# A streaming kernel's loads issued earlier, and another gate for its first store

## The chip, the cores and the metric

The kernel runs on one core of one Trainium2 chip. The core's VectorE (DVE in the profile) does the arithmetic, SyncE (SP) issues the transfers between HBM and the on-chip memory, and 16 DMA engines carry them out. TensorE (PE) does one tiny matmul; ScalarE does nothing. The metric is the device time of one execution in microseconds (us), the median of several runs.

## The reference

The reference scales one array by a scalar and adds it to another, in bf16:

```python
B, S, D = 512, 32, 640
x, fx: (B, S, D) bf16;  alpha: (1,) bf16
def reference(x, fx, alpha):
    return x + alpha * fx
```

Each array has 10,485,760 elements, 20.97 MB. Two are read and one is written, 62.9 MB in all, with one multiplication and one addition per element.

## The kernel before

All three arrays are seen as 128 partitions by 160 *units* of K = 512 columns (1 KB per partition and unit, so 128 KB per unit). On the chip there is one tile, `room`, with 207 such units per partition (`ROOM`, line 13); x and fx together are 320 units, so places are used more than once. x and the result share a place: the add is done in place.

What is done, and in which order, is written by hand in the string `PLAN` (lines 25 to 50). A loop (line 100) takes its steps in order, and each goes to the end of its engine's own queue: loads and stores to SP's, multiplies and adds to VectorE's. Engines run their queues in order and independently; a step waits on its engine until what it needs is done, and the steps behind it on that engine wait too. The steps are:

- `x a b @ p` or `f a b @ p`: load units a to b of x or fx to place p (line 94);
- `a`: load alpha and spread it to 128 partitions with a matmul (`spread_alpha`, lines 82 to 89);
- `m p n`: multiply the n units at place p by alpha, in place (line 108);
- `+ p q n`: add the n units of fx at place q to the n units of x at place p (line 113);
- `s a b @ p`: store units a to b from place p (line 94). With `after x 128` it also waits until the load of x that starts at unit 128 has landed (lines 95 and 96).

A load into a place that held something else waits for the add that read it last. Before, the loads run in this order: fx 0-64 (in two parts, alpha behind them), x 0-32, x 32-64, fx 64-128, x 64-88, x 88-128, fx 128-160, x 128-152, x 152-160. The first five wait for nothing. x 64-88 goes where the first 24 units of fx lay and so waits for the add of x 0-32; x 88-128 waits for the add of x 32-64; fx 128-160 goes to places 64 to 96 and waits for `+ 143 79 24`; x 128-152 and x 152-160 go to places 96 to 128 and wait for `+ 167 103 25`. The stores, of units 0-64, 64-128 and 128-160, come last; the first has the gate `after x 128`. At the end SP waits for all transfers.

A transfer of 128 partitions is done by all 16 DMA engines, each with eight of the rows; the trace has one packet for each row.

Of the kernel before, what the change touches and what calls it, by code (L numbers as in the profile page):

```python
# [1 line left out]

# [4 lines left out]

ALU = mybir.AluOpType
F32 = mybir.dt.float32

K = 512
P = 128
ROOM = 207

PLAN = """
f 0 8 @ 143
f 8 64 @ 151
a
x 0 32 @ 0
m 143 64  # L30
x 32 64 @ 32
+ 0 143 32
+ 32 175 32
f 64 128 @ 79
m 79 64
x 64 88 @ 143
+ 143 79 24
x 88 128 @ 167
f 128 160 @ 64
+ 167 103 25  # L40
+ 192 128 15
x 128 152 @ 96
x 152 160 @ 120
m 64 32
s 0 64 @ 0 after x 128
+ 96 64 24
s 64 128 @ 143
+ 120 88 8
s 128 160 @ 96
"""  # L50


@with_exitstack
def kernel(
    ctx: ExitStack,
    tc: tile.TileContext,
    x: bass.AP,
    fx: bass.AP,
    alpha: bass.AP,
    out: bass.AP,  # L60
):
    nc = tc.nc
    whole = {
        name: t.flatten_outer_dims().rearrange("(p n) d -> p (n d)", p=P)
        for name, t in (("x", x), ("f", fx), ("s", out))
    }
    assert whole["x"].shape[1] == 160 * K

    consts = ctx.enter_context(tc.tile_pool(name="consts", bufs=1))
    psum = ctx.enter_context(tc.tile_pool(name="psum", bufs=1, space=bass.MemoryType.PSUM))  # L70
    rooms = ctx.enter_context(tc.tile_pool(name="rooms", bufs=1))
    ctx.enter_context(tc.manual_schedule())

    room = rooms.tile([P, ROOM * K], x.dtype, name="room")
    a_f = consts.tile([P, 1], F32, name="a_f")
    info = mybir.DependencyInfo(mybir.DependencyClass.Sync, mybir.DependencyReason.DATA)
    done, moved = [], {}

    def units(t, a, b):
        return t[:, a * K : b * K]  # L80

    def spread_alpha():
        a_1 = consts.tile([1, 1], alpha.dtype, name="a_1")
        done.append(nc.sync.dma_start(out=a_1[:], in_=alpha[None, :]))  # L84
        ones = consts.tile([1, P], alpha.dtype, name="ones")
        nc.vector.memset(ones[:], 1.0)  # L86
        a_ps = psum.tile([P, 1], F32, name="a_ps")
        done.append(nc.tensor.matmul(a_ps[:], ones[:], a_1[:], start=True, stop=True))  # L88
        nc.vector.tensor_copy(out=a_f[:], in_=a_ps[:])  # L89

    def transfer(what, a, b, at, after):
        away, here = units(whole[what], a, b), units(room, at, at + b - a)
        out, in_ = (away, here) if what == "s" else (here, away)
        r = nc.sync.dma_start(out=out, in_=in_)  # L94
        if after:
            tc.add_manual_dep(r.ins, moved[after].ins.name, info, reason="issued late")
        moved[what, a] = r
        done.append(r)

    for step in PLAN.strip().split("\n"):  # L100
        what, *rest = step.split()
        if what == "a":
            spread_alpha()
        elif what == "m":
            t, n = map(int, rest)
            f = units(room, t, t + n)
            done.append(
                nc.vector.tensor_scalar(out=f, in0=f, scalar1=a_f[:], scalar2=None, op0=ALU.mult)  # L108
            )
        elif what == "+":  # L110
            t, u, n = map(int, rest)
            xt, f = units(room, t, t + n), units(room, u, u + n)
            done.append(nc.vector.tensor_tensor(out=xt, in0=xt, in1=f, op=ALU.add))  # L113
        else:
            a, b, _, at = rest[:4]
            after = (rest[5], int(rest[6])) if len(rest) > 4 else None
            transfer(what, int(a), int(b), int(at), after)

    last = nc.sync.nop(nofuse=True)
    for i in done[:-1]:  # L120
        tc.add_manual_dep(last.ins, i.ins.name, info, reason="all but the last store")


# [1 line left out]
_INS = ['x', 'fx', 'alpha']  # L125
_OUTS = [((512, 32, 640), 'bfloat16')]


# [23 lines left out]
```

## Time and profile before

| | us |
|---|---|
| median of 3 runs (lowest, highest) | 152.31 (152.21, 152.66) |
| the profiled execution | 152.51 |
| its span in the profile | 150.7 |
| busy in the span: VectorE | 65.8 (44%) |
| adds: 128x16384 / 128x12288 / 128x4096 | 8.693 / 6.559 / 2.284 each |
| multiplies: 128x32768 / 128x16384 | 8.752 / 4.480 each |
| moved: read / written | 41.94 MB / 20.97 MB, 417 GB/s over the span |

The span is the stretch that the profiler records; the device time has some 1.8 us more around it. Times in the profile are counted from the span's start. In the profile's rows SPq is SP's queue, "room<-in_x_dram" a load of x, "out_dram<-room" a store, and a bracket at the end of a row tells how long the engine stood idle before it and what ended that. Rows of the timeline merge neighbours of a kind: "x2" with a length can span two instructions that lie apart.

### The profile page before, as it was taken

The numbers are of one execution on the slowest core, as the hardware profiler recorded it, in microseconds if no ns is written. First come the engines' busy times: TensorE is split into PE (matmuls) and PEld (weight loads), VectorE is DVE, ScalarE is ACT, GpSimd is POOL, SyncE is SP. The second block draws the span as 40 slices with busy tenths as digits, with TensorE's granted clock in tenths as the row PEclk, the third lists the DMA queues.
The fourth block names the chain that finished last, engine by engine and source line by source line (L and its number), as shares of the span: only waits on it lengthen the run. The fifth ranks groups of instructions, "written<-read, shape, count | busy, mean of one in ns | idle before, by whom it ended". The sixth has DMA issues, their size and how long they took to land.

```text
span 150.7 us, 83 instructions
## 1 busy us (share of the span) xinstructions
PE 0.2 (0%) x1; PEld 0.1 (0%) x1; DVE 65.8 (44%) x12; POOL 0.2 (0%) x4
## 2 busy tenths in 40 slices
PE   0000000000000000000000000000000000000000
PEld 0000000000000000000000000000000000000000
DVE  0000009979889400799935999479500000000000
POOL 0000000000000000000000000000000000000000
DMA  5997989999969696999999999999799697979992
GB/s 170 596 411 320 487 383 426 435 461 461 565 296 557 278 557 285 437 489 424 435 435 417 417 389 430 400 450 504 330 504 557 296 539 330 504 330 391 417 478 104
DMA packets 1874, 62.92 MB, mean 417 GB/s; under 512 B 210, under 2 KB 210, under 8 KB 210
## 3 DMA queue, kind: packets, MB, share of 16 engines
q1 hardware_dynamic: 1874, 62.92, 97.3%
HBM read 41.94 MB, written 20.97 MB: 417 GB/s over the span
## 4 chain that ended last, share of the span: by engine, by line
DMA 54%; DVE 15%; DVEq 1%; SPq 1%; issue 0%
DMA room<-in_x_dram 54%; DVE room L113 15%; DVEq L147 1%; SPq L94 1%; SPq L84 0%; DVEq L113 0%
## 5 line engine op out<-in xcount | busy, mean ns | idle before, releaser
L113 DVE TENSOR_TENSOR room<-room 128x16384 bf16<-128x16384 bf16 (+4 forms) x7 | 43.6, 6252 | 8.8 <-DMA room<-in_x_dram 8.8
L108 DVE TENSOR_SCALAR room<-room,a_f 128x32768 bf16<-128x32768 bf16 (+1 forms) x3 | 22.0, 7328 | 10.7 <-DMA room<-in_fx_dram 10.7
L89 DVE COPY a_f<-a_ps 128x1 f32<-128x1 f32 x1 | 0.2, 159 | 21.5 <-PE a_ps L88 21.5
L86 DVE MEMSET ones<- 1x128 bf16 x1 | 0.2, 165 | 0.8 <-PEq L136 0.8
L88 PE MATMUL a_ps<-a,ones 1*128 1x1 bf16 x1 | 0.2, 158 | 22.3 <-DMA a<-in_alpha_dram 22.3
L136 POOL MEMSET const-bfloat16-1.0<- 128x1 bf16 x1 | 0.1, 102 | 0.0
L136 POOL MEMSET const-uint8-127<- 128x1 uint8 x1 | 0.1, 102 | 0.0
L88 PEld LDWEIGHTS <-ones 1*128 1x128 bf16 x1 | 0.1, 101 | 1.0 <-DVE ones L86 1.0
L136 POOL MEMSET const-float32-0.0<- 128x1 f32 x1 | 0.1, 99 | 0.2 <-issue 0.2
L136 POOL MEMSET const-float32-1.0<- 128x1 f32 x1 | 0.1, 99 | 0.0
## 6 DMA issues: line engine op xcount, KB each, us to landing
room<-in_x_dram SPq DMA_DIRECT2D x2, 4096.0 KB, 34.8
room<-in_fx_dram SPq DMA_DIRECT2D x1, 7168.0 KB, 21.3
room<-in_x_dram SPq DMA_DIRECT2D x2, 3072.0 KB, 19.4
room<-in_x_dram SPq DMA_DIRECT2D x1, 5120.0 KB, 30.0
room<-in_fx_dram SPq DMA_DIRECT2D x1, 4096.0 KB, 13.8
out_dram<-room SPq DMA_DIRECT2D x1, 4096.0 KB, 42.3
room<-in_fx_dram SPq DMA_DIRECT2D x1, 1024.0 KB, 4.8
room<-in_x_dram SPq DMA_DIRECT2D x1, 1024.0 KB
```

The lines of the kernel that those rows point to most:

```text
L86: nc.vector.memset(ones[:], 1.0)
L88: done.append(nc.tensor.matmul(a_ps[:], ones[:], a_1[:], start=True, stop=True))
L89: nc.vector.tensor_copy(out=a_f[:], in_=a_ps[:])
L94: r = nc.sync.dma_start(out=out, in_=in_)
L108: nc.vector.tensor_scalar(out=f, in0=f, scalar1=a_f[:], scalar2=None, op0=ALU.mult)
L113: done.append(nc.vector.tensor_tensor(out=xt, in0=xt, in1=f, op=ALU.add))
L136: nc = _bacc.Bacc("TRN2", target_bir_lowering=False, num_devices=1)
L147: with _tile.TileContext(nc) as tc:
```

## The change

Only the order and the division of the steps change; the places, the bytes and the arithmetic are the same.

- x 0-64 is loaded in one transfer instead of two.
- The adds of x 0-64 become 24, 16 and 24 units, and behind each the load into the place that it frees is issued: x 64-88, x 88-104, x 104-128 (before: 24 and 40 units, behind adds of 32 and 32).
- The adds of x 64-128 become 17, 7, 16, 9, 9 and 6 units (before 24, 25 and 15). fx 128-160 waits for the one of 17 units. x 128-160 is one load (before two) and waits for those of 7, 16 and 9; the last 9 + 6 units come behind the multiply of fx 128-160.
- The first store waits for the add `+ 192 128 9` instead of the landing of x 128-152; to allow this, adds are recorded in `moved` as transfers are.
- The last adds, of 24 and 8 units, become one of 32.

```diff
 a
-x 0 32 @ 0
+x 0 64 @ 0
 m 143 64
-x 32 64 @ 32
-+ 0 143 32
-+ 32 175 32
 f 64 128 @ 79
++ 0 143 24
+x 64 88 @ 143
++ 24 167 16
+x 88 104 @ 167
++ 40 183 24
+x 104 128 @ 183
 m 79 64
-x 64 88 @ 143
-+ 143 79 24
-x 88 128 @ 167
++ 143 79 17
 f 128 160 @ 64
-+ 167 103 25
-+ 192 128 15
-x 128 152 @ 96
-x 152 160 @ 120
++ 160 96 7
++ 167 103 16
++ 183 119 9
+x 128 160 @ 96
 m 64 32
-s 0 64 @ 0 after x 128
-+ 96 64 24
++ 192 128 9
+s 0 64 @ 0 after + 192
++ 201 137 6
 s 64 128 @ 143
-+ 120 88 8
++ 96 64 32
 s 128 160 @ 96
...
-            done.append(nc.vector.tensor_tensor(out=xt, in0=xt, in1=f, op=ALU.add))
+            moved[what, t] = nc.vector.tensor_tensor(out=xt, in0=xt, in1=f, op=ALU.add)
+            done.append(moved[what, t])
```

## The prediction

> **What bounds the kernel now.** I read the page first: busy shares, the DMA slices, the queue, the chain of waits.
>
> ```profile
> span 150.7 us, 83 instructions
> PE 0.2 (0%) x1; PEld 0.1 (0%) x1; DVE 65.8 (44%) x12; POOL 0.2 (0%) x4
> DMA  5997989999969696999999999999799697979992
> q1 hardware_dynamic: 1874, 62.92, 97.3%
> DMA 54%; DVE 15%; DVEq 1%; SPq 1%; issue 0%
> ```
>
> VectorE works 44% of the span; the 16 DMA engines are occupied 97.3% of it. So only time in which a DMA engine stands idle or is slow can be won, and the chain's 15% of VectorE matters only where an engine ran dry behind it. The question is where the missing 2.7% lies. Then the timeline, for the moments at which SP issues transfers and what releases them:
>
> ```profile
> 41.01 9.98 SPq L94 DMA_DIRECT2D room<-in_x_dram  x2
> 61.28 8.75 DVE L108 TENSOR_SCALAR room<-room,a_f 128x32768 bf16<-128x32768 bf16 x1 [10.65 <-DMA room<-in_fx_dram]
> 76.65 0.33 SPq L94 DMA_DIRECT2D room<-in_fx_dram  x1
> 80.71 10.89 DVE L113 TENSOR_TENSOR room<-room 128x12800 bf16<-128x12800 bf16 x2 [4.08 <-DMA room<-in_x_dram]
> 87.56 0.80 SPq L94 DMA_DIRECT2D room<-in_x_dram  x2
> 98.80 9.20 SPq L94 DMA_DIRECT2D out_dram<-room  x3
> 98.88 8.76 DVE L113 TENSOR_TENSOR room<-room 128x12288 bf16<-128x12288 bf16 x2 [2.88 <-DMA room<-in_x_dram]
> ```
>
> x 64-88 (41.01) and x 88-128 (50.66, merged into the first row) are issued long before fx 64-128 has landed at 61.3. But fx 128-160 goes out at 76.65, while its turn comes at 79.6-80.2, and x 128-152 at 87.56 for a turn at 89.4-90.0. Last, DMA shares by window (a packet counts where it starts; last columns are clock, DMA share, GB/s):
>
> ```profile
> 41.00:60.00 19.00, 0.00 (x0) 0.00 (x0) 8.69 (x1) 0.00 (x0) 1.00 1.00 435
> 89.30:91.30 2.00, 0.00 (x0) 0.00 (x0) 2.00 (x1) 0.00 (x0) 1.00 0.95 381
> 98.80:99.30 0.50, 0.00 (x0) 0.00 (x0) 0.42 (x1) 0.00 (x0) 1.00 0.91 360
> 148.50:149.70 1.20, 0.00 (x0) 0.00 (x0) 0.00 (x0) 0.00 (x0) 1.00 0.00 0
> ```
>
> With a deep queue the engines give 435 GB/s; around 90 and 99 they fall short; after 148.5 no packet starts any more though the last ends at 149.64. The trace's single packets (one row of a transfer each; I chained each packet to the one that ended just before it) say who falls short:
>
> ```
>                       13 engines        3 engines
> fx 128-160 ends       89.38-89.96       89.58, 89.62, 89.67
> x 128-152 starts      2 ns later        90.22, 90.47, 90.51; first packet 1.47-1.63, others 0.91
> x 152-160 ends        99.15-99.8        about 101.0, 101.28, 101.32
> first store starts    99.64-99.80       100.99, 101.29, 101.32
> last store has landed 148.49-148.68     149.63, 149.95, 149.98
> ```
>
> Three engines found no descriptors of x 128-152 when they were done with fx 128-160: 0.6-0.9 us of idleness and a first packet 0.56-0.72 us too long, 1.3 to 1.5 us in all. They never make it up, since no engine has spare time afterwards, and the kernel ends with them, 1.30 us (149.98 - 148.68) after the other 13. These 13 lost less: they ran out of loads up to 0.64 us before the first store, which waited for x 128-152 to land (98.78) and went out at 98.80.
>
> **The change, part by part.** The profiled execution took 152.51 us, span 150.7 and 1.8 around it; the median of the runs is 152.31, 0.20 lower, so differences are taken in the span and put on 152.31.
>
> Prices of an add: 128x16384 took 8.693 and 128x4096 took 2.284, so 0.148 us plus 0.5216 ns per column: 6.56 for 24 units of 512, 4.69 for 17, 4.42 for 16, 2.55 for 9, 2.02 for 7, 1.75 for 6. Multiplies: 8.75 for 64 units, 4.48 for 32. Seven adds become ten: 3 x 0.148 = 0.44 us more on VectorE, which is idle over half the span.
>
> *x 0-64 in one load.* One issue less at 2.4 (0.56 us of SP), behind fx 8-64, which keeps the engines busy to 22: no effect there. But the first add can no longer start at 32.29 with half of x; it starts when all has landed, at 41.9. From there: 24 units to 48.5, 16 to 52.9, 24 to 59.5. So x 64-88, 88-104 and 104-128 are issued at 48.5, 52.9, 59.5; their turns come at 60.2, 67.5 and 72.3. The cover is fx 64-128, in flight to 61.3: leads of 11.7 us and more, where 3.5 (below) are the most that was needed, so the later first add may slip 8 us more before it costs.
>
> *fx 128-160 and x 128-160.* The multiply of fx 64-128 starts at 61.28 as now (VectorE free at 59.5), ends 70.0; 17 units to 74.7: fx 128-160 is issued at 74.7 instead of 76.65, lead 4.9 us instead of 3.0. Then 7 units to 76.8, 16 to 81.2, 9 to 83.8 (x 104-128 lands at 80.7, in time): x 128-160 is issued at 83.8 instead of 87.56, lead 5.6 us instead of 1.8. The small delays at the start of fx 128-160 now (one gap of 0.10, two first packets 0.17 too long) fall on engines that end with the 13 or are swallowed in the later stall, so that lead is worth 0 to 0.1. Both leads, 4.9 (the thinnest margin) and 5.6 us, exceed the longest delay seen from issue to an undisturbed rate: x 128-152 in the three engines, (90.51 + 0.56) - 87.56 = 3.5 us. So this stall goes: 1.30 us for the end of the three.
>
> *The gate of the first store.* fx 128-160 lands at 90.4 as now; its multiply ends at 94.9, the gating add of 9 units at 97.5, and SP issues the store then, 1.3 us earlier than now and 1.6 to 2.1 us before the engines run out of loads (99.1-99.65: 9.7 us after 89.4-89.96). Queued behind the gate on SP are only the other two stores: the second wants the 6 units that end at 99.3, the third the last add, from about 100.1 to 108.8; the queue then holds 64 units of stores each time (the second store's own last landing is 140 now), so neither is missed. What the 13 engines lose now (0 to 0.64 idle, first store packets 2.48 instead of 2.42) goes or stays at 0.06. The price of a late descriptor for a store issued into full reading is in no row: bounds below.
>
> *Packets.* x 0-64 and x 128-160 need 8 packets per engine less each, x 64-128 8 more; one packet of 65536 B took 2.418 against 2 x 1.215: 0.012 us each, 8 fewer are 0.1 us at most; I take 0.05.
>
> Sum: -1.30 (three engines) - 0.1 (part of what the 13 lose; the last of them found its store with no gap, so between 0 and 0.2) - 0.05 = -1.45 us. 152.31 - 1.45 = 150.86.
>
> **Bounds of the unknown price.** Store descriptors now: the 13 engines that stood waiting began 0.84 to 1.0 us after the issue, and the other three found theirs ready when they wanted them, 2.2 to 2.5 us after it. With 1.6-2.1 us of lead this is a stall of 0 to 0.5. The upper end is the load of 87.56, whose three late engines began 2.66-2.95 us after the issue and were at full rate after 3.4-3.5: 97.5 + 2.7..3.5 against the 99.35 in the middle is 0.8 to 1.65. I take 0, since a store's own rows are nearer than a load's; both ends go into the range.
>
> **The rivals.**
> *The store's wait takes the load's place.* The lead of the first store (1.6-2.1) is that of x 128-152 now (1.8-2.4), at the same full reading. If three engines are as late for it, 0.8 to 1.65 of the 1.45 come back: 151.66 to 152.5. Against it: the store rows above.
> *The lag has nothing to do with the lead* (it hangs on the addresses of x 128, or on three of the engines): then x 128-160 stalls all the same and only the 0.05 and the earlier store remain: about 152.2. For it: 13 engines had their descriptors within 1.8 us. Against it: the 3.0 us lead of fx 128-160 left only 0.1-0.17, leads of 19 us and more left nothing, and the three engines' later packets are as short as the others'.
> The Trainium skill speaks for this rival (DMA: Bandwidth & Descriptors, "Latency and other measured facts"): about 0.6 us to the first byte of a transfer issued by SP, by which 1.8 us of lead would be enough and the early issue would buy nothing. The trace disagrees for the three engines (2.66 us and more); the same section's 2 us of HBM latency under high load, added to 0.6 as an estimate, comes to 2.6.
> *Slower: the gated store comes too late.* The gate hangs on the landing of fx 128-160 plus 7.1 us of VectorE, with everything else already issued. If descriptors of a store issued among full reads need more than 97.5 to 101.3 = 3.8 us on some engine, the end is as late as now or later; at 4.5 us, 150.86 + (102.0 - 99.35) = 153.5. For it: nothing that long is seen; against it: 3.5 is the longest.
>
> **How the numbers follow.** A measurement here can tell about 0.3% (0.46 us): faster is below 151.85, slower above 152.77. Forecast 0.53 (own range 150.6-151.4); store's wait 0.25, half of it below 151.85; lag without the lead 0.11; slower 0.11. Faster 0.53 + 0.12 = 0.65, same 0.13 + 0.11 = 0.24, slower 0.11. The range 150.6 to 152.4 leaves out the last case and the far end of the second.
>
> **What would show it.** In the profile after: x loads issued at 48.5, 52.9, 59.5, fx at 74.7, x 128-160 at 83.8, first store near 97.5; all 16 engines starting x 128-160 without a gap near 89.4-90; the last landings of all within 0.6 us of each other near 148.5, the span near 149.3. Wrong would be: gaps in some engines after 99.1 (the store), or a first packet of x 128-160 of over 1.3 us (the lag without the lead), or VectorE still adding when a load's turn comes.

## The result, and the profile after

The changed kernel takes 150.82 us (median of 4 runs, 150.75 to 150.87); the kernel before, with one more run beside it, 152.49 (152.21 to 152.90). The ratio is 0.9888, with a 95% interval of 0.9862 to 0.9914: faster by about 1.1%. The forecast was 150.86. The profiled execution took 150.81 us, its span 149.0, against 152.51 and 150.7.

The page of the changed kernel, the same parts as were shown of before (busy time, DMA share of 40 slices, the queue, the chain that ended last):

```profile
span 149.0 us, 85 instructions
PE 0.2 (0%) x1; PEld 0.1 (0%) x1; DVE 65.9 (44%) x15; POOL 0.2 (0%) x4
DMA  5997996969899796999998999999696969697994
q1 hardware_dynamic: 1730, 62.92, 98.1%
DMA 38%; DVE 32%; another core or an unknown queue 1%; SPq 1%; issue 0%; DVEq 0%
```

The bytes are the same and the DMA engines' share of the span rises from 97.3 to 98.1%. VectorE's part of the chain doubles, 15% to 32%, while the kernel gets faster. The chain follows who released whom, and the first store is now released by an add; that doesn't mean that any DMA engine waited for this add. Whether an engine ran dry is seen only in the DMA records.

The timeline of the changed kernel, the moments of issue (start, length, queue, transfer):

```profile
41.70 17.36 DVE L115 TENSOR_TENSOR room<-room 128x12288 bf16<-128x12288 bf16 x3 [10.34 <-DMA room<-in_x_dram]
48.29 11.13 SPq L96 DMA_DIRECT2D room<-in_x_dram  x3
61.00 8.75 DVE L110 TENSOR_SCALAR room<-room,a_f 128x32768 bf16<-128x32768 bf16 x1 [1.94 <-DMA room<-in_fx_dram]
74.51 0.33 SPq L96 DMA_DIRECT2D room<-in_fx_dram  x1
83.25 0.33 SPq L96 DMA_DIRECT2D room<-in_x_dram  x1
97.25 11.86 SPq L96 DMA_DIRECT2D out_dram<-room  x3
```

VectorE starts adding 9.4 us later than before, and it costs nothing: its three adds are done 1.94 us before fx 64-128 has landed. fx 128-160 goes out at 74.5 and x 128-160 at 83.25, 5 and 6 us ahead of their turns.

Windows, first of before and then of the changed kernel, over the stretch in which x 128-160 is read (last columns: clock, DMA share, GB/s):

```profile
89.30:99.10 9.80, 0.00 (x0) 0.00 (x0) 6.92 (x3) 0.00 (x0) 1.00 0.97 407
```

```profile
89.30:99.10 9.80, 0.00 (x0) 0.00 (x0) 8.62 (x3) 0.00 (x0) 1.00 1.00 428
148.50:149.70 1.20, 0.00 (x0) 0.00 (x0) 0.00 (x0) 0.00 (x0) 1.00 0.00 0
```

407 GB/s became 428 there: the short windows of the prediction (2 us and less) are no good for a comparison, because a packet counts where it starts and a whole row of 16 may fall on either side of an edge. After 148.5 no packet starts in either kernel; only the records of single packets tell how long the last ones run. Those of the changed kernel, in the form of the prediction's table:

```
                      all 16 engines
fx 128-160 ends       89.39-89.73
x 128-160 starts      at most 4 ns later; first packet 1.21-1.25, in one engine 1.44
x 128-160 ends        99.13-99.61
first store starts    at most 4 ns later; first packet 2.42 (once 2.44)
last store has landed 147.84-148.27
```

Between 5 us and its end no engine is idle for more than 0.08 us at a time, and no group of three lags: the last landings lie within 0.43 us where they lay within 1.49.

### The profile page after: what moved, and what is told of

It reads as the page before. It is cut to its first block, busy times and chain, and to the rows that moved or that the text cites. A ratio compares the mean times of both kernels' runs of the same rounds, so it can differ in the third digit from the quotient of the medians.

```text
span 149.0 us, 85 instructions
## 1 busy us (share of the span) xinstructions
PE 0.2 (0%) x1; PEld 0.1 (0%) x1; DVE 65.9 (44%) x15; POOL 0.2 (0%) x4
## 3 DMA queue, kind: packets, MB, share of 16 engines
q1 hardware_dynamic: 1730, 62.92, 98.1%
## 4 chain that ended last, share of the span: by engine, by line
DMA 38%; DVE 32%; another core or an unknown queue 1%; SPq 1%; issue 0%; DVEq 0%
DMA room<-in_x_dram 38%; DVE room L115 27%; DVE room L110 6%; SPq L96 1%; SPq L86 0%; DVEq L115 0%
## 5 line engine op out<-in xcount | busy, mean ns | idle before, releaser
L115 DVE TENSOR_TENSOR room<-room 128x12288 bf16<-128x12288 bf16 (+6 forms) x10 | 43.7, 4419 | 11.5 <-DMA room<-in_x_dram 11.5
```

Source lines behind the costliest of these rows:

```text
L115: moved[what, t] = nc.vector.tensor_tensor(out=xt, in0=xt, in1=f, op=ALU.add)
```

## The experiments

Each run is compared with the kernel before on the same chip. There its median was 152.8 to 152.9 over 16 to 20 runs, a little above the 152.49 of the first comparison, so the ratios are what to compare. The engines' gaps and long packets come from the single packets of each run's trace, chained as in the prediction. The records don't name the engine, so an engine can be followed within a run but not from run to run. "Too long" is against the usual time of such a packet, 1.21 us for 32 KB and 0.31 us for 8 KB.

**One part alone.** The kernel before, with only the division that lets x 128-152 go out early:

```diff
-x 88 128 @ 167
+x 88 104 @ 167
+x 104 128 @ 183
...
-+ 167 103 25
++ 167 103 16
++ 183 119 9
 + 192 128 15
```

> The kernel before with one part of the change alone: x 88-128 is loaded as 16 and 24 units and the add of 25 units divided into 16 and 9, so that x 128-152 can be issued near 83.7 instead of 87.6. x 0-64 in two loads, the lead of fx 128-160 (3.0) and the store's old gate stay. If the lead of x 128-152 decides: no stall near 90, the three engines are not late, x 128-152 lands near 97.6 and the store goes out then, 150.8 to 151.1. If the lag hangs on addresses or engines, or the gain on the other parts: 152.2 to 152.5.

Measured: 151.22 us, ratio 0.9891 (0.9852 to 0.9931), the whole gain. The issues of this run:

```profile
76.66 0.33 SPq L96 DMA_DIRECT2D room<-in_fx_dram  x1
83.46 0.80 SPq L96 DMA_DIRECT2D room<-in_x_dram  x2
97.82 0.82 SPq L96 DMA_DIRECT2D out_dram<-room  x2
```

x 128-152 goes out at 83.46 instead of 87.56; no engine has a gap near 90, the last landings lie within 0.43 us. The lead of fx 128-160 is the old 3 us and the store's gate the old one. That gate works here since x 128-152 lands while x 152-160 still runs. So x 0-64 in one load, the earlier fx 128-160 and the new gate together added nothing that can be measured beyond this division.

**The load late again, everything else kept.** The changed kernel with x 128-160 behind the add that ends near 87.5 (multiplies are recorded in `moved` too, so that the store can wait for one):

```diff
-x 128 160 @ 96
-m 64 32
 + 192 128 9
-s 0 64 @ 0 after + 192
 + 201 137 6
+x 128 160 @ 96 after + 201
+m 64 32
+s 0 64 @ 0 after m 64
```

> The changed kernel, but x 128-160 (one load) waits for the add of the last 6 units, so it is issued near 87.5 as before the change instead of 83.3; the first store waits for the multiply of fx 128-160 (94.8), so its lead is over 4 us and not in question. If the lead of the load decides: some engines (three before) find no descriptors near 89.4-90, start 0.5 to 0.9 us late with a first packet 0.5 too long, and the time is 152.0 to 152.4. If the stall came from two loads issued one behind the other, or if the gain came from the store's gate: no stall, 150.7 to 150.9.

Measured: 154.07 us, ratio 1.0091 (1.0061 to 1.0121). The stall came back: issued at 87.67, five engines started x 128-160 up to 0.75 us late with first packets 0.5 to 0.8 too long. But the loss was larger than either forecast: from 97.1 on the last two packets of x 128-160 took 3.4 to 4.0 us together instead of 2.43, in 14 engines (the chains of the other two can't be told apart there). Both stores had been issued from 95.11, and lay behind these packets. To separate the two, adds of used-up places (9 and 6 units) were put behind the multiply, as gates for stores at the changed kernel's times; the edit is to the run just told:

```diff
 m 64 32
-s 0 64 @ 0 after m 64
++ 128 128 9
+s 0 64 @ 0 after + 128
++ 137 137 6
-s 64 128 @ 143
+s 64 128 @ 143 after + 137
```

> The late load of x 128-160 (issued near 87.6) once more, now with both first stores issued at the changed kernel's own times: two adds of dead places on VectorE (9 and 6 units of fx that have been used up) stand behind the multiply of fx 128-160 and gate the stores at 97.5 and 99.3. The earlier late-load run had a second disturbance: loads of 1.8 to 2.8 us instead of 1.21 on all 16 engines from 97.1 on, 2 us after both stores were issued at 95.1 and 95.5. If that was the stores' doing and the load's lead costs what it cost before the change: some engines stall near 90 by 1.0 to 1.5 us, no slow loads at 97, 152.0 to 152.5. If the lead alone costs everything: 153.5 to 154.1 again, slow loads at 97 included.

Measured: 154.03 us, ratio 1.0091 (1.0061 to 1.0120): a miss for the lower forecast. The higher one has the time right, but the slow packets at 97 that it went with are nearly gone. The load and the first store in this run's timeline:

```profile
87.66 0.33 SPq L98 DMA_DIRECT2D room<-in_x_dram  x1
97.54 0.35 SPq L98 DMA_DIRECT2D out_dram<-room  x1
```

Near the end only the late engines still store, in this run's windows:

```profile
149.00:150.00 1.00, 0.00 (x0) 0.00 (x0) 0.00 (x0) 0.00 (x0) 1.00 0.38 164
```

With stores at 97.54 and 99.2, five engines began 0.5 to 1.4 us late, with first packets 0.3 to 1.2 too long. In the other eleven the packets at 97 are 0.3 too long at most, though in eight of them a packet that began near 92 took 0.4 to 0.5 too long, which no forecast had. In the five the last packet but one takes 1.0 to 1.2 us too long; it began between 98.5 and 99.7, and the other eleven began to store between 99.8 and 100.7. The eleven have landed by 149.34, the five between 150.72 and 151.77.

Whether two smaller loads soften the stall was tried in the same arrangement:

```diff
-x 128 160 @ 96 after + 201
+x 128 152 @ 96 after + 201
+x 152 160 @ 120
```

> The late load with gated stores once more (issue near 87.6, stores at 97.5 and 99.3, adds of used-up places as gates), now with x 128-160 in two loads of 24 and 8 units as the kernel before has it. The one whole late load cost 154.0, 1.1 more than the kernel before at the same lead. If the division of the load is what softens the stall: near the kernel before, 152.5 to 153.1. If the division is of no weight: 153.7 to 154.2.

Measured: 153.68 us, ratio 1.0052 (1.0030 to 1.0074). Here too engines start up to 1.4 us late, four of them, and the kernel stays above the one before. So the division of the load does not explain why the kernel before was better than these. Whether it takes off a part of the loss (1.0091 became 1.0052) stays open, since the intervals overlap.

**How much lead is enough.** The same arrangement with the load behind 2 of the last 6 units:

```diff
-+ 201 137 6
++ 201 137 2
 x 128 160 @ 96 after + 201
++ 203 139 4
```

> The same with x 128-160 in one load, issued behind only 2 of the last 6 units, near 86.7: a lead of about 2.8 us instead of 1.9. If the lead that is needed lies near the 3.0 that fx 128-160 had (gaps of 0.1, first packets 0.2 long, no cost): 151.0 to 151.6. If the stall grows steadily with the missing lead from 4.9 down: 152.0 to 153.

Measured: 151.42 us, ratio 0.9897 (0.9864 to 0.9931). The issue in this run's timeline:

```profile
86.61 0.33 SPq L99 DMA_DIRECT2D room<-in_x_dram  x1
```

That is 2.9 us before the first engine's turn: three engines are touched, with gaps of 0.22 and 0.13 and first packets 0.22, 0.65 and 0.11 too long. One microsecond more of lead than in the late run with the stores held back, and with the stores issued at the same times, took away nearly all of the loss.

**Two loads, but early.**

```diff
-x 128 160 @ 96
+x 128 152 @ 96
+x 152 160 @ 120
```

> The changed kernel with x 128-160 in two loads (24 and 8 units, as before the change), both issued near 83.3. If the lead decides: 150.8 to 150.9, no stall (8 packets per engine more are 0.1 us at most). If the division in two small loads made the stall: 152.0 to 152.4.

Measured: 151.15 us, ratio 0.9884 (0.9844 to 0.9923), no gap near 90. The division made no stall.

**The store's gate.** The old gate in the changed kernel, where x 128 is now one load:

```diff
-s 0 64 @ 0 after + 192
+s 0 64 @ 0 after x 128
```

> The changed kernel with the old gate of the first store (the landing of x that starts at unit 128, now the whole of x 128-160, near 100.0). If engines that have run out begin a store 0.85 us after its issue: all 16 idle from 99.1-99.6 to 100.85, 1.2 to 1.7 us, time 152.1 to 152.5: then the new gate is needed for the gain though it gave little by itself. If the gate is of no weight: 150.8.

Measured: 152.59 us, ratio 0.9979 (0.9956 to 1.0001), nearly the whole gain lost. The store is issued in this run's timeline when the load has landed:

```profile
100.29 0.82 SPq L96 DMA_DIRECT2D out_dram<-room  x2
100.36 8.69 DVE L115 TENSOR_TENSOR room<-room 128x16384 bf16<-128x16384 bf16 x1 [1.08 <-DMA room<-in_x_dram]
```

All 16 engines start it between 101.13 and 101.29, 0.84 to 1.00 us after the issue, and have stood idle for 1.30 to 1.95 us each. With x 128-160 in one load the new gate is needed; with two loads the old one did as well.

The other way, no gate at all:

```diff
-s 0 64 @ 0 after + 192
+s 0 64 @ 0
```

> The changed kernel without a gate: the first store is issued right behind x 128-160, near 83.7; the second at 99.3. If the lead of a store is harmless as that of a load is: 150.8. If a store in the queue slows loads: slow load packets from about 85.7 on or at the last two loads of each engine, 151.5 to 154.

Measured: 151.60 us, ratio 0.9903 (0.9873 to 0.9934). There are no gaps, but the last packet of x 128-160 takes 0.1 to 0.7 us too long in all 16 engines; nothing before it is slow, though the store had been issued at 83.94. A gate between the two,

```diff
-s 0 64 @ 0 after + 192
+s 0 64 @ 0 after m 64
```

> The changed kernel with its first store gated by the multiply of fx 128-160 (issued near 94.8 instead of 97.3); the second store still waits for the last 6 units (99.3), the load stays early. If a store that lies in the queue while loads run slows the last loads: packets of x 128-160 of over 1.5 us from about 97, time 151.5 to 153. If only two stores issued one behind the other do that, or a late load: 150.8, no slow packet.

gave 151.54 us, ratio 0.9897 (0.9858 to 0.9936): issued at 95.08, the last packet 0.1 to 0.65 too long in 12 of the 16 engines. By the ratios both lie 0.2 to 0.4 us above the two kernels with an early load whose store went out near 97.6 (0.9884 for the early load divided, 0.9878 for both stores at once, below). The intervals overlap, so by the times alone this isn't shown; the long packets are plain, and those two kernels have none. In the kernel before the gate did more:

```diff
-s 0 64 @ 0 after x 128
+s 0 64 @ 0
```

> The kernel before without its gate: stores issued near 88.5 and 91.5, the loads late as they are. If stores in the queue are harmless: the three engines lag as before and set the end, the 13 others lose their idle time of up to 0.64, which nobody sees: 152.3 to 152.9, the same as before. If a store in the queue slows loads: 153 to 154.5.

Measured: 153.70 us, ratio 1.0053 (1.0030 to 1.0075). Four engines are late as in the others (gaps of 0.5 to 1.5 near 91), and in each engine several of the eight packets of x 152-160 are 0.1 to 0.7 us too long (one 0.9). How much of the loss is the longer gaps and how much the slow packets is not separated here.

**Both stores at once.**

```diff
++ 201 137 6
 m 64 32
 + 192 128 9
 s 0 64 @ 0 after + 192
-+ 201 137 6
```

> The changed kernel with the last add of 6 units moved ahead of the multiply of fx 128-160, so that the second store is issued right behind the first (near 97.5 and 97.9 instead of 99.4). If two stores in the queue slow the last loads where one does not: load packets of over 1.4 us from 98, 151.5 to 152.2. If only the time since the first store's issue counts: 150.8 to 151.2, no slow packet.

Measured: 151.11 us, ratio 0.9878 (0.9843 to 0.9913), no slow load. With the first store at 97.59 the second one right behind it does no harm.

**A try for more.** alpha first, and fx 0-64 in one load:

```diff
-f 0 8 @ 143
-f 8 64 @ 151
 a
+f 0 64 @ 143
```

> The changed kernel with alpha first and fx 0-64 in one load instead of 8 and 56 units. The first packets of 8 KB take 0.1 to 0.7 us too long on each engine now, until about 3 us; 8 packets per engine fewer are 0.1 us at most. If the slow start is a price per packet: up to 0.3 us faster, 150.5 to 150.7. If it is a price of the first data whatever their size, or alpha ahead delays the first load by its issue (0.33): 150.8 to 151.2.

Measured: 151.75 us, ratio 0.9923 (0.9900 to 0.9947), some 0.6 us worse than the pair of stores, on the same chip. The first packets start at 2.13 instead of 1.73, since alpha is issued first, so 0.4 us is that; and each engine's first packet, now of 64 KB, takes 0.3 to 1.5 us too long, where those of 8 KB took up to 0.7 in the changed kernel. The slow start is not a price per packet that fewer packets save.

No run beat the changed kernel clearly: 0.9878 for the pair of stores lies inside its interval.

## Why the prediction was right

**The place.** The three lagging engines were read from the packets of before, and put down to a load issued 1.8 us ahead of its turn. The division alone (0.9891) gave all of the gain, the late load alone took it away, and 1 us more of lead brought nearly all of it back. The rival, by which the stall comes whatever the lead, falls with these: the addresses and the 16 engines are the same, only the lead differs. It is also not three engines each time: four or five in the late runs. Whether the same ones are late each time can't be read, since the packets don't name their engine.

**The size.** The forecast was 1.45 us. The spans differ by 1.71 (150.73 to 149.02), the last landings as well (149.98 to 148.27). The lag of the three engines behind the other 13 is 1.30 of it, as was summed. The latest of the 13 moved too, by 0.41 (148.68 to 148.27), where the sum had 0.15. Some of that is no work of the change: when fx 128-160 ended, the changed kernel's engines were already ahead, by 0.06 on the mean and by 0.23 in the latest. So 0.18 to 0.35 is left for what had 0.15. The sum also took the idle time of the 13 before the first store for a loss of its own, and it was the same stall once more: the gate waited for x 128-152 in all engines, and its last packets ended at 98.23 to 98.44 in the three late ones, at 97.26 and less in the others. In the run of the division alone, with the same gate, they ended by 97.38, the store went out at 97.82, and no engine ran dry. That the forecast median, 150.86, lies 0.04 us from the measured one owes something to luck, since the median taken for before was 152.31 and moved to 152.49 with one more run.

**The unknown price.** The first store had 1.9 to 2.4 us of lead, and it was an open question whether it would stall as the load did. It didn't: no gap in any engine, first packets 2.42. The choice of the store's own rows against the load's was right. The rival of a gated store that comes too late is refuted as well, with 97.25 against 97.5 expected. But the upper bound taken from the load, 3.5 us from issue to full rate, was too low for loads: 87.66 to 91.17 + 1.18 is 4.7 us in the worst engine of the late run. The changed kernel's leads of 5 and 6 us were long enough; leads cut to 3.5 by that bound were not tried, and at 2.9 three engines were still touched.

**What was costed at nothing.** The first add 9.4 us later, three more adds, the earlier fx 128-160: all rightly, as the division alone shows. The earlier store was given up to 0.2 us, and the sum said nothing of why a gate should be there at all. The runs with an earlier store show it: issued about 2 us before the loads end (97.25), it slows no packet; issued 4.5 us before (95.08) or earlier, it slows the last one. Nothing between was tried.

The Trainium skill (DMA: Bandwidth & Descriptors, "Latency and other measured facts") gives about 0.6 us to the first byte. Here idle engines needed 0.84 to 1.00 us from the start of SP's issue, which itself takes 0.35, so 0.5 to 0.65 from its end, and for them the trace agrees. Some that had been reading needed 2.7 and more; by 0.6 the old lead would have been ample, and the runs decide against it.

## What to carry to other kernels

When the DMA engines are busy 97% of the span, look for what is left in the records of single packets: a few engines that stall once are late to the end, because no engine has time to catch up, and the kernel ends with them. Ask also which other step waits for all engines, since it waits for the late ones too. Issue a load some 5 us before the queue runs out of work (5 and 6 us cost nothing here, 2.9 still cost about 0.3 us), here by dividing the step that frees its place, and don't go by the time in which an idle engine starts. A store that is to follow loads wants to be issued neither when the last load has landed (1.30 to 1.95 us idle) nor long before (0.1 to 0.7 us on the last packet of most engines), but about 2 us before the loads end.

## What the runs showed that was not expected

- The delay from issue to start depends on what the engine is doing. An idle engine begins 0.84 to 1.00 us after the issue. With all engines reading, most have the next load in time at a lead of 1.8 us, and three to five of the 16 don't: in the kernel before and in the two late runs with the stores held back they reached full rate, counting the extra time of the first packet, 3.3 to 4.7 us after the issue. Why some do and others don't stays open.
- The times of the kernel with the stall scatter more: the kernel before took 152.25 to 153.95 us in 18 runs on one chip and 152.36 to 153.46 in 16 on another, the changed kernel 150.75 to 150.87 in 4, the kernel before with the division alone 151.12 to 151.44 in 4. That the stall differs between executions would explain it, as would the smaller number of runs in part. On a third chip the kernel before once took 151.14, about what it takes with the division; whether that execution went without the stall isn't known.
- Stores issued well ahead of their turn slow the loads before them: only the last packet of a load, by 0.1 to 0.7 us, with one store behind an early load; the last two, by 1.0 to 1.6 us together, with both stores issued from 95.1 on and a late load. That the five late engines of the second late run lost 1.0 to 1.2 us in their last packet but one fits this, their stores having waited since 97.5, and would tell why these kernels came out above the one before, whose store waited for a landing at 98.8. It was not tried by itself: the other engines' beginning to store at that time would do as a cause too. Their storing as such is less likely: once all the others stored, the packets of the late engines took the usual time again, with one exception of 0.1 us, in this run, in the late load divided and in the kernel before.
